# Attention and a gated unit on one core: keys without padding on TensorE's row halves, and turns and casts done by transfers

## The chip, the cores and the metric

One core of one Trainium2 chip. The metric is the device time of one launch in microseconds (us). The kernel before takes 296.35 us, the median of three runs (295.74 to 299.75).

## What is computed

Grouped-query attention over 8 batches, 16 query heads in 4 groups, 384 tokens and 64 numbers per head, and then a gated unit on the heads laid side by side (x, 384 x 1024 per batch):

```python
scores = scale * np.matmul(q, k.transpose(0, 1, 3, 2))
attn = np.exp(scores - max); attn = attn / sum
x = attn @ v                                  # heads side by side: 384 x 1024
h = np.maximum(x @ w_in, 0.0)                 # 1024 -> 1024
u, v = h[..., :512], h[..., 512:]
v_n = (v - mean(v)) / np.sqrt(var(v) + 1e-06)
v_s = einsum('ts,bsd->btd', w_spatial, v_n) + b_spatial[None, :, None]
out = (u * v_s) @ w_out                       # 512 -> 1024
```

Inputs and output are float32; the kernel multiplies in float16 and adds up in float32.

## The kernel before, in words

Tokens are dealt to partitions as token = 3p + t, so that one partition's row of a head is one piece in memory, and three tiles t of 128 tokens make up a sequence.

**Attention.** SP loads q, k and v (L75). POOL casts them to float16 (`cast_k`, `cast_q`, `cast_v`, L177 to L194), batch 0 in part on DVE. TensorE turns k and q by multiplying with an identity, six 128x128 blocks at a time into one PSUM buffer (L205, L225), and DVE copies them out (L216, L235). A pair is two query heads of two neighbouring key groups: head A lies on rows 0 to 63, head B on rows 64 to 127. The keys are kept twice in `kz`, once with zeros on the lower rows and once on the upper, so that a matmul over all 128 rows gives one head's scores. `scores` (L251) does two such matmuls of 384 queries into one PSUM tile, and ACT takes the exp of both at once (L258, 768 columns). 24 such units make a batch. `weigh` (L267) multiplies each 128x128 block of exps with the 64 values and a column of ones; `normalize` (L281, L282) divides by that column on DVE. `x_transposes` (L296) turns x on TensorE and DVE copies it out (L301).

**Gated unit.** `gated_unit` is a generator that yields after each matmul. Per batch: v = x @ w_in for three token tiles (pv, L312, 24 matmuls of 512 columns), relu and statistics on DVE (L321 to L324), u for four column tiles (pu, L332, 32 matmuls of 384 columns) with relu on ACT (L340), normalisation of v on POOL (vn, L350), the product with w_spatial (psp, L362 and L365) in which a matmul of ones with the bias comes first, the product with u on DVE (gT, L373), and out (po, L380, 24 matmuls of 512 columns) that DVE and ACT copy out by halves (L389). SP stores.

**Order.** Scheduling is by hand. The main loop runs over the units n of all batches; each step emits the next unit's scores, the jobs booked with `at(n, ...)`, the weighing that has come due, and as many matmuls of the gated unit of the batch before as a 24th of a batch's columns. Batch 0's gated unit begins at n = 29. Each engine works its queue in that order. The weights w_in and w_out are loaded by SP into three staging buffers (L120, L137) and cast by POOL (L131, L145).

PSUM: two score tiles of two banks, one bank for the weighing, three buffers of one bank (`ps_ck`) for everything else.

Of the kernel before, what the change touches and what calls it, by code (L numbers as in the profile page):

```python
# [17 lines left out]
def kernel(  # L18
# [15 lines left out]
    P = 128  # L34
# [6 lines left out]
    NPAIR = HQ // 2  # L41
# [4 lines left out]
    VW = D + 2  # L46

# [3 lines left out]
    wst = ctx.enter_context(tc.tile_pool(name="wst", bufs=3))  # L51
    ld = ctx.enter_context(tc.tile_pool(name="ld", bufs=2))
    att = ctx.enter_context(tc.tile_pool(name="att", bufs=3))
# [5 lines left out]
    ps_ck = ctx.enter_context(tc.tile_pool(name="ps_ck", bufs=3, space=PSUM))  # L59
# [9 lines left out]
    )  # L69

# [3 lines left out]
    def part(name, src, t, lo, hi, eng=None):  # L74
        (eng or nc.sync).dma_start(  # L75
            t[:, lo:hi, :], src[lo:hi].rearrange("h (p t) d -> p h (t d)", t=NT)
        )

    def stage_tile(n, b, j=None):
        if n == "q":  # L80
            t = ld.tile([P, 2 * G, NT * D], FP32, name=f"q32_{b}_{j}", tag="q32")
            stage[n, b, j] = t
            return t
        t = ld.tile([P, HKV, NT * D], FP32, name=f"{n}32_{b}", tag=f"{n}32")
        stage[n, b] = t
        return t

    def load_k(b):
        part("k", k[b], stage_tile("k", b), 0, HKV)

    def load_v(b):
        part("v", v[b], stage_tile("v", b), 0, HKV)

    def load_q(b, j):
        part("q", q[b, 8 * j : 8 * j + 8], stage_tile("q", b, j), 0, 2 * G)


    k0, v0, q00 = stage_tile("k", 0), stage_tile("v", 0), stage_tile("q", 0, 0)
    part("q", q[0, 0:8], q00, 0, 2, nc.scalar)
    part("k", k[0], k0, 0, 2)  # L100
    part("q", q[0, 0:8], q00, 4, 6)
    part("v", v[0], v0, 0, 2)
    part("q", q[0, 0:8], q00, 2, 4)
    part("q", q[0, 0:8], q00, 6, 8)
    part("k", k[0], k0, 2, 4)
    part("v", v[0], v0, 2, 4)
    load_q(0, 1)

    w_in16 = cst.tile([P, NPAIR, DFF], FP16, name="w_in16")
    w_out16 = cst.tile([P, NM, DM], FP16, name="w_out16")  # L110
    wsT16 = cst.tile([P, NT, S], FP16, name="wsT16")

    w_stage = {}

    def load_w_in(j, half):

        t = wst.tile([P, G, DH], FP32, name=f"wi32_{j}_{half}", tag="w32")
        for hh in range(2):
            r0 = (8 * j + 4 * hh) * D
            nc.sync.dma_start(  # L120
                t[hh * D : (hh + 1) * D],
                moe_w_in[r0 : r0 + G * D, half * DH : (half + 1) * DH].rearrange(
                    "(i d) f -> d i f", i=G
                ),
            )
        w_stage["in", j, half] = t

    def cast_w_in(j, half, engs):
        t = w_stage.pop(("in", j, half))
        for i in range(G):  # L130
            engs[i % len(engs)].tensor_copy(  # L131
                w_in16[:, G * j + i, half * DH : (half + 1) * DH], t[:, i]
            )

    def load_w_out(c):
        t = wst.tile([P, 2, DM], FP32, name=f"wo32_{c}", tag="w32")
        nc.sync.dma_start(  # L137
            t, moe_w_out[2 * c * P : 2 * (c + 1) * P, :].rearrange("(m p) f -> p m f", p=P)
        )
        w_stage["out", c] = t  # L140

    def cast_w_out(c, engs):
        t = w_stage.pop(("out", c))
        for i in range(2):
            engs[i % len(engs)].tensor_copy(w_out16[:, 2 * c + i], t[:, i])  # L145


    ident = cst.tile([P, P], FP32, name="ident")
    make_identity(nc, ident)
    ident16 = cst.tile([P, P], FP16, name="ident16")  # L150
    nc.vector.tensor_copy(ident16, ident)
    eps_t = cst.tile([P, 1], FP32, name="eps_t")
    nc.vector.memset(eps_t, 1e-6)
    kz = [cst.tile([P, 2, 2, S], FP16, name=f"kz{i}") for i in range(2)]
    v1 = [cst.tile([P, HKV, NT, VW], FP16, name=f"v1_{i}") for i in range(2)]
    for i in range(2):
        for j in range(2):
            eng = nc.vector if i == 0 and j == 0 else nc.gpsimd
            eng.memset(kz[i][D:P, 0, j], 0.0)
            eng.memset(kz[i][0:D, 1, j], 0.0)  # L160
        nc.gpsimd.memset(v1[i][:, :, :, D:VW], 1.0)
    ones_b = cst.tile([P, P], FP16, name="ones_b")
    nc.gpsimd.memset(ones_b, 0.0)
    nc.gpsimd.memset(ones_b[0:1, :], 1.0)
    nc.gpsimd.memset(ones_b[32:33, :], 1.0)
    bias_b = cst.tile([P, S], FP16, name="bias_b")
    nc.gpsimd.memset(bias_b, 0.0)


    k16s, q16s = {}, {}  # L170

    def cast_k(b, eng, js=(0, 1)):
        if b not in k16s:
            k16s[b] = ld.tile([P, 2, NT, 2, D], FP16, name=f"k16_{b}", tag="k16")
        src = stage["k", b].rearrange("p (j h) (t d) -> p j h t d", h=2, t=NT)
        for hh in range(2):
            eng.tensor_copy(  # L177
                k16s[b][:, js[0] : js[-1] + 1, :, hh, :], src[:, js[0] : js[-1] + 1, hh]
            )

    def cast_v(b, eng, js=(0, 1)):
        g0, g1 = 2 * js[0], 2 * js[-1] + 2
        eng.tensor_copy(
            v1[b % 2][:, g0:g1, :, 0:D].rearrange("p g t d -> p (g t) d"),
            stage["v", b][:, g0:g1].rearrange("p g (t d) -> p (g t) d", t=NT),
        )

    def cast_q(b, j, eng, parts=1):
        t = ld.tile([P, G, NT, 2, D], FP16, name=f"q16_{b}_{j}", tag="q16", bufs=4)
        src = stage.pop(("q", b, j)).rearrange("p (h i) (t d) -> p h i t d", h=2, t=NT)  # L190
        n = G // parts
        for c in range(parts):
            for hh in range(2):
                eng.tensor_copy(  # L194
                    t[:, c * n : c * n + n, :, hh, :].rearrange("p i t d -> p (i t) d"),
                    src[:, hh, c * n : c * n + n].rearrange("p i t d -> p (i t) d"),
                )
        q16s[b, j] = t


    def k_transposes(b, js=(0, 1)):
        ps = ps_ck.tile([P, len(js), S], FP16, name=f"kps_{b}_{js[0]}", tag="ck")
        for x, j in enumerate(js):
            for t in range(NT):
                nc.tensor.transpose(  # L205
                    ps[:, x, t * P : (t + 1) * P],
                    k16s[b][:, j, t].rearrange("p h d -> p (h d)"),
                    ident16,
                )
        z = kz[b % 2]  # L210
        for hh in range(2):
            dst, src = z[hh * D : (hh + 1) * D, hh, js[0] : js[-1] + 1], ps[hh * D : (hh + 1) * D]
            if b == 0 and js == (0,) and hh:
                nc.scalar.copy(dst, src)
            else:
                nc.vector.tensor_copy(dst, src)  # L216

    qTs = {}

    def q_transposes(b, c):  # L220
        ps = ps_ck.tile([P, 2, S], FP16, name=f"qps_{b}_{c}", tag="ck")
        t16 = q16s[b, c // 2]
        for i in range(2):
            for t in range(NT):
                nc.tensor.transpose(  # L225
                    ps[:, i, t * P : (t + 1) * P],
                    t16[:, 2 * (c % 2) + i, t].rearrange("p h d -> p (h d)"),
                    ident16,
                )
        qT = att.tile([P, 2, S], FP16, name=f"qT_{b}_{c}", tag="qT")  # L230
        if b == 0 and c == 0:
            nc.scalar.copy(qT[:, 0], ps[:, 0])  # L232
            nc.vector.tensor_copy(qT[:, 1], ps[:, 1])
        else:
            nc.vector.tensor_copy(qT, ps)  # L235
        qTs[b, c] = qT


    aTs, avs, x16s, xts = {}, {}, {}, {}

    def scores(n):
        b, r = divmod(n, 24)
        pair, u = divmod(r, 3)
        j = pair // G
        if u == 0:
            aTs[b, pair] = att.tile([P, 6, S], FP16, name=f"aT_{b}_{pair}", tag="aT")
        aT = aTs[b, pair]
        sc = ps_sc.tile([P, 2, 512], FP32, name=f"sc_{b}_{pair}_{u}", tag="sc")
        for i in range(2):
            hh, t = divmod(2 * u + i, NT)  # L250
            nc.tensor.matmul(  # L251
                sc[:, i, 0:S],
                kz[b % 2][:, hh, j, t * P : (t + 1) * P],
                qTs[b, pair // 2][:, pair % 2, :],
                start=True,
                stop=True,
            )
        nc.scalar.activation(aT[:, 2 * u : 2 * u + 2, :], sc[:, :, 0:S], AF.Exp, scale=scale)  # L258
# [45 lines left out]
    def gated_unit(b):  # L304
# [70 lines left out]
        for tt in range(NT):  # L375
# [16 lines left out]
            if not last:  # L392
                nc.sync.dma_start(rows[:, tt, :], osb)
# [164 lines left out]
```

## Time and profile before

| | |
|---|---|
| median of three runs | 296.35 us |
| span of the profiled execution | 297.9 us |
| TensorE busy | 277.2 us (93%) |
| ACT, DVE, POOL busy | 182.7, 164.1, 76.8 us |
| moved by transfers | 38.75 MB, mean 130 GB/s |
| first score matmul starts | 8.46 us |
| last w_in load lands | 43.8 us |
| last po matmul ends | 294.1 us |

The span is from the first to the last instruction of one execution; the runs' times lie around it. A busy share is an average over stages with different limits, so the windows of a stage are read next to it. Matmul ends in the profile are modelled, so that a matmul's mean duration is longer than the pace at which one follows the other; the chain in order of time gives that pace.

### The profile page before, as it was taken

The page shows a single profiled execution, that of the slowest core. Times are in us where ns is not written, and L with a number is a line of the kernel's source. Part 1 is how long each engine was busy: PE and PEld are TensorE (multiplying, and loading weights), DVE is VectorE, ACT ScalarE, POOL GpSimd, SP SyncE. Part 2 cuts the span into 40 slices and gives each one's busy share as a digit, 9 for nine tenths or more (in the row PEclk, how much of TensorE's full clock was granted, in tenths as well). Part 3 has the DMA queues.
Part 4 walks back from the last instruction along what each step waited for, and adds up shares of the span by engine and source line. Part 5 has one row for each costly group of instructions (what it writes and reads, how often), then busy time and mean ns, then how long its engine had stood idle before and what let it go on. Part 6 is the DMA issues. An engine that isn't in the chain of part 4 may idle for free.

```text
span 297.9 us, 6566 instructions
## 1 busy us (share of the span) xinstructions
PE 277.2 (93%) x2745; PEld 174.8 (59%) x2745; DVE 164.1 (55%) x358; ACT 182.7 (61%) x267; POOL 76.8 (26%) x123
## 2 busy tenths in 40 slices
PE   1888766999999999999999999999999999999994
PEld 1566433666566666666566656666566666665451
DVE  4356460556474656656474665656474665646641
ACT  1889632576757666776757666676757666673122
POOL 6433549693004230062003230062003000030030
PEclk9999995999999999999999999999999999999999
DMA  7999999813590037600491036600400032002305
GB/s 222 302 217 215 223 273 379 260 23 123 180 312 8 2 139 214 179 0 28 181 284 44 0 144 207 183 2 18 195 4 0 2 136 78 2 0 78 135 1 211
DMA packets 31951, 38.75 MB, mean 130 GB/s; under 512 B 1201, under 2 KB 25778, under 8 KB 31922
## 3 DMA queue, kind: packets, MB, share of 16 engines
q1 hardware_dynamic: 31650, 38.15, 42.3%
q8 instruction: 21, 0.34, 0.5%
q10 hardware_dynamic: 272, 0.20, 0.2%
q14 instruction: 8, 0.07, 0.1%
HBM read 25.76 MB, written 12.58 MB: 129 GB/s over the span
## 4 chain that ended last, share of the span: by engine, by line
PE 82%; DMA 11%; SPq 3%; POOL 2%; DVE 1%; issue 1%; ACT 0%; DVEq 0%; POOLq 0%
PE sc L251 17%; PE pu L332 14%; PE po L380 14%; PE pv L312 13%; PE av L267 10%; DMA wi<-in_moe_w_in_dram 9%; PE psp L365 5%; PE xps L296 3%; PE qps L225 3%; SPq L75 2%; PE psp L362 2%; POOL w_in L131 1%; DMA q<-in_q_dram 1%; PE kps L205 1%; POOL ws L420 1%; SPq L120 1%
## 5 line engine op out<-in xcount | busy, mean ns | idle before, releaser
L258 ACT ACTIVATE aT<-sc 128x768 f16<-128x768 f32 x192 | 153.5, 810 | 87.3 <-PE sc L251 87.1
L251 PE MATMUL sc<-qT,kz 128*128 128x384 f16 x384 | 95.4, 332 | 3.4 <-ACT qT L232 2.4
L267 PEld LDWEIGHTS <-aT 128*128 128x128 f16 x1152 | 53.4, 98 | 17.1 <-issue 0.7
L267 PE MATMUL av<-v,aT 128*128 128x65 f16 x1152 | 57.2, 194 | 0.0
L350 POOL TENSOR_SCALAR vn<-vr,rstd,nmr 128x512 f16<-128x512 f32 x24 | 18.2, 773 | 150.5 <-DVE nmr L345 130.8
L332 PE MATMUL pu<-xt,w_in 128*128 128x384 f16 x256 | 50.9, 326 | 0.0
L312 PE MATMUL pv<-w_in,xt 128*128 128x512 f16 x192 | 50.8, 386 | 0.0
L380 PE MATMUL po<-w_out,gT 128*128 128x512 f16 x192 | 49.2, 379 | 0.1
L251 PEld LDWEIGHTS <-kz 128*128 128x128 f16 x384 | 34.4, 99 | 23.9 <-issue 3.8
L282 DVE TENSOR_TENSOR x<-av,r 128x384 f16<-128x384 f32 x64 | 35.7, 557 | 2.2
L235 DVE COPY qT<-qps 128x768 f16<-128x768 f16 x31 | 17.1, 551 | 27.0 <-PE qps L225 27.0
L281 DVE RECIPROCAL r<-av 128x6 f32<-128x6 f32 x64 | 12.5, 195 | 34.9 <-PE av L267 33.8
L332 PEld LDWEIGHTS <-w_in 128*128 128x128 f16 x256 | 22.7, 98 | 12.7 <-issue 0.3
L194 POOL CAST q<-q 128x768 f16<-128x768 f32 x30 | 24.0, 830 | 8.0 <-DMA q<-in_q_dram 8.0
L380 PEld LDWEIGHTS <-gT 128*128 128x128 f16 x192 | 16.8, 97 | 15.6 <-DVE gT L373 2.4
L312 PEld LDWEIGHTS <-xt 128*128 128x128 f16 x192 | 16.6, 99 | 13.5 <-issue 0.9
L365 PE MATMUL psp<-wsT,vn 128*128 128x384 f16 x96 | 24.2, 326 | 0.0
L389 DVE COPY osb<-po 128x512 f32<-128x512 f32 x24 | 16.5, 689 | 13.2 <-PE po L380 13.2
L373 DVE TENSOR_TENSOR gT<-psp,uT 128x384 f16<-128x384 f32 x32 | 17.1, 553 | 11.5 <-PE psp L365 11.3
L321 DVE TENSOR_SCALAR vr<-pv 128x512 f32<-128x512 f32 x24 | 16.5, 688 | 12.4 <-PE pv L312 12.2
L301 DVE COPY xt<-xps 128x768 f16<-128x768 f16 x32 | 17.6, 551 | 6.6 <-PE xps L296 5.3
L389 ACT COPY osb<-po 128x512 f32<-128x512 f32 x24 | 14.0, 581 | 10.5 <-PE po L380 10.5
(50 smaller groups left out, 186.6 us busy)
## 6 DMA issues: line engine op xcount, KB each, us to landing
q<-in_q_dram SPq DMA_DIRECT2D x15, 768.0 KB, 8.6
out_dram<-osb SPq DMA_DIRECT2D x21, 512.0 KB, 2.8
wi<-in_moe_w_in_dram SPq DMA_DIRECT2D x8, 512.0 KB, 15.3
k<-in_k_dram SPq DMA_DIRECT2D x7, 384.0 KB, 5.1
v<-in_v_dram SPq DMA_DIRECT2D x7, 384.0 KB, 5.5
wo<-in_moe_w_out_dram SPq DMA_DIRECT2D x2, 1024.0 KB, 13.5
out_dram<-osb SPq DMA_DIRECT2D x6, 256.0 KB, 2.0
q<-in_q_dram SPq DMA_DIRECT2D x3, 192.0 KB, 3.9
```

Of the source, the lines that this page charges most:

```text
L194: eng.tensor_copy(t[:, c * n : c * n + n, :, hh, :].rearrange("p i t d -> p (i t) d"), src[:, hh, c * n : c * n + n].rearrange("p i t d -> ...
L251: nc.tensor.matmul(sc[:, i, 0:S], kz[b % 2][:, hh, j, t * P : (t + 1) * P], qTs[b, pair // 2][:, pair % 2, :], start=True, stop=True,)
L258: nc.scalar.activation(aT[:, 2 * u : 2 * u + 2, :], sc[:, :, 0:S], AF.Exp, scale=scale)
L267: nc.tensor.matmul(av[:, hh, qt, :], aT[:, hh * NT + t, qt * P : (qt + 1) * P], v1[b % 2][:, g, t, 0 : D + 1], start=(t == 0), stop=(t == ...
L282: nc.vector.tensor_tensor(x16s[b][:, :, pair * P : (pair + 1) * P].rearrange("p t (h d) -> p h t d", h=2), av[:, :, :, 0:D], r.to_broadcas ...
L301: nc.vector.tensor_copy(xts[b][:, 2 * c : 2 * c + 2, :], ps)
L312: nc.tensor.matmul(pv, xt[:, kt, st * P : (st + 1) * P], w_in16[:, kt, DH:DFF], start=(kt == 0), stop=(kt == NPAIR - 1),)
L332: nc.tensor.matmul(pu[:, 0:S], w_in16[:, kt, m * P : (m + 1) * P], xt[:, kt, :], start=(kt == 0), stop=(kt == NPAIR - 1),)
L350: nc.gpsimd.tensor_scalar(vn, v_r[st], rstd[:, st : st + 1], nmr[:, st : st + 1], op0=ALU.mult, op1=ALU.add,)
L365: nc.tensor.matmul(psp[:, 0:S], v_n[st][:, m * P : (m + 1) * P], wsT16[:, st, :], start=False, stop=(st == NT - 1),)
L380: nc.tensor.matmul(po, gT[:, m, tt * P : (tt + 1) * P], w_out16[:, m, half * 512 : (half + 1) * 512], start=(m == 0), stop=(m == NM - 1),)
L389: (nc.scalar.copy if half else nc.vector.tensor_copy)(osb[:, cols], po)
```

## The change

- Keys are no longer padded. A set is one tile of 128 queries of four heads in each of two groups. A unit is one tile of 128 keys against 512 queries (four heads) for each of two groups: the one group's keys and queries lie on rows 0 to 63, the other's on rows 64 to 127, and each group's matmul runs over its 64 rows into a PSUM bank of its own. ACT takes the exp of 1024 columns at once. 18 units make a batch, and they are emitted two at a time, so that nine steps make a batch.
- From batch 2 on (for x from batch 1 on) q, k and x are turned by SP's transposing transfers from SBUF to SBUF (`k_send`, `q_send`, `x_send`); so is w_spatial. Batches 0 and 1 are still turned on TensorE.
- w_in and w_out are loaded and cast in one transfer each part, issued by POOL, straight into the float16 tiles; the staging buffers and POOL's casts go.
- The bias is spread to all partitions by a transfer and added by DVE (`vs`); the product with u moves to POOL. The bias matmuls go.
- The statistics enter POOL's normalisation as mean and rstd, so that DVE's step for the negative product goes.
- po is copied out by DVE alone, but for the last batch.
- Batch 0's gated unit begins within batch 0, by token tiles; the others wait for step 7 and step 11 of their batch (the `("from", n)` yields).
- PSUM: `ps_av` takes two banks, `ps_ck` has two buffers instead of three.

```diff
+    SETS = 2 * NT
+    UNITS = NT * SETS
+    STEPS = UNITS // 2
...
-    ps_ck = ctx.enter_context(tc.tile_pool(name="ps_ck", bufs=3, space=PSUM))
+    ps_ck = ctx.enter_context(tc.tile_pool(name="ps_ck", bufs=2, space=PSUM))
...
+    def load_w_in(half, lo, hi):
+        cols = slice(half * DH, (half + 1) * DH)
+        pool.dma_start(
+            w_in16[:, lo:hi, cols],
+            moe_w_in[lo * P : hi * P, cols].rearrange("(t p) f -> p t f", p=P),
+        )
...
+    def k_send(b):
+        new_kT(b)
+        sp.dma_start_transpose(
+            kTs[b].rearrange("p j (t c) -> p (j t) c", t=NT),
+            k16s[b].rearrange("p j t h d -> p (j t h d)"),
+        )
+
+    def q_send(b, j):
+        new_qT(b, j)
+        sp.dma_start_transpose(
+            qTs[b, j].rearrange("p t (i c) -> p (t i) c", i=G),
+            q16s[b, j].rearrange("p t i h d -> p (t i h d)"),
+        )
...
+    def unit(u):
+        b, r = divmod(u, UNITS)
+        s, kt = divmod(r, NT)
+        qt, j = divmod(s, 2)
...
+        sc = ps_sc.tile([P, 2, G * P], FP32, name=f"sc_{b}_{s}_{kt}", tag="sc")
         for hh in range(2):
+            rows = slice(hh * D, (hh + 1) * D)
             nc.tensor.matmul(
+                sc[:, hh, :],
+                kTs[b][rows, j, kt * P : (kt + 1) * P],
+                qTs[b, j][rows, qt, :],
                 start=True,
                 stop=True,
             )
+        act.activation(aTs[b, s][:, kt], sc, AF.Exp, scale=scale)
...
+    def x_send(b, qt):
+        if qt == 0:
+            new_xt(b)
+        sp.dma_start_transpose(
+            xts[b][:, :, qt * P : (qt + 1) * P], x16s[b][:, qt]
+        )
...
+        if b == 0:
+            for st in range(NT):
+                yield ("from", 3 * st + 5)
+                yield from v_part(st)
+                if st == NT - 1:
+                    norm()
+                yield from u_part(st)
+        else:
+            yield ("from", b * STEPS + 7)
+            yield from v_part(0)
+            yield from v_part(1)
+            yield ("from", b * STEPS + 11)
+            yield from v_part(2)
+            yield from u_cols()
...
-            nc.tensor.matmul(psp[:, 0:S], ones_b, bias_b, start=True, stop=False)
-            yield S
...
-            nc.vector.tensor_tensor(gT[:, m, :], psp[:, 0:S], uT[:, m, :], ALU.mult)
+            vs = moe.tile([P, S], FP32, name=f"vs_{b}_{m}", tag="vs", bufs=4)
+            dve.tensor_tensor(vs, psp[:, 0:S], bias_bc, ALU.add)
+            pool.tensor_tensor(gT[:, m, :], vs, uT[:, m, :], ALU.mult)
...
+    for b in range(2, B):
+        s0 = STEPS * b
+        at(s0 - 12, load_k, b)
+        at(s0 - 12, load_v, b)
+        at(s0 - 11, load_q, b, 0)
+        at(s0 - 10, load_q, b, 1)
+        at(s0 - 8, cast_k, b, pool)
+        at(s0 - 7, cast_q, b, 0, pool)
+        at(s0 - 6, k_send, b)
+        at(s0 - 5, q_send, b, 0)
+        at(s0 - 5, cast_q, b, 1, pool)
+        at(s0 - 3, q_send, b, 1)
+        at(s0 - 2, cast_v, b, pool)
...
+    for n in range(total + 1):
+        for u in (2 * n, 2 * n + 1):
+            if u < UNITS * B:
+                unit(u)
...
+        sets = ends.pop(n, [])
+        owed = pour(n, owed + STEP - len(sets) * WEIGH)
+        for b, s in sets:
+            weigh(b, s)
+            if s % 2 and b:
+                x_send(b, s // 2)
```

`v_part`, `u_part` and `u_cols` emit pv and pu, the first by token tiles and the last by column tiles. With a step's units come the jobs booked for it, then the gated unit's matmuls, then the weighing that has come due. The order of TensorE's queue in a steady batch is, for the stretch that the prediction speaks of: the sixth weighing, a burst of two units, three and eight pv matmuls, a burst, the eight pv matmuls of the third token tile.

## The prediction

> **What bounds the kernel now.** I read the totals first, then the strip of slices, then the windows of one steady batch, and last the chain of waits inside that batch. The totals put the span at 297.9 us; 297.9 is 1.5 us above the median of the runs shown (296.35), so my sum is made against the span and 1.5 us is taken off at the end.
>
> ```profile
> PE 277.2 (93%) x2745; PEld 174.8 (59%) x2745; DVE 164.1 (55%) x358; ACT 182.7 (61%) x267; POOL 76.8 (26%) x123
> ...
> PE   1888766999999999999999999999999999999994
> ...
> PEclk9999995999999999999999999999999999999999
> DMA  7999999813590037600491036600400032002305
> GB/s 222 302 217 215 223 273 379 260 23 123 180 312 8 2 139 214 179 0 28 181 284 44 0 144 207 183 2 18 195 4 0 2 136 78 2 0 78 135 1 211
> ```
>
> From the eighth slice to the end TensorE has no gap, while transfers have many. Before that, transfers are full and TensorE is not: the load of inputs and weights sets the first 50 us. The windows, one per batch, show the steady part (PE, weight loads, DVE, ACT, POOL, clock, transfer share, GB/s):
>
> ```profile
> 44.70:57.00 12.30, 8.95 (x64) 5.20 (x65) 3.65 (x9) 3.27 (x5) 11.99 (x17) 0.72 1.00 333
> ...
> 109.60:143.17 33.57, 33.57 (x344) 21.46 (x342) 19.98 (x43) 22.64 (x34) 7.10 (x10) 1.00 0.37 119
> 143.17:176.74 33.57, 33.57 (x344) 21.47 (x342) 19.97 (x43) 22.64 (x34) 7.10 (x10) 1.00 0.38 119
> ```
>
> A batch takes 33.57 us and all of it is TensorE. ACT and DVE have 11 and 14 us to spare. The chain in order of time gives the pace of each kind of matmul without the modelled ends:
>
> ```profile
> 143.17 0.86 PE po L380 x4
> 144.04 0.33 PE sc L251 x2
> ...
> 145.33 0.28 PE av L267 x9
> ...
> 146.48 0.34 PE qps L225 x6
> ```
>
> So 512 columns cost 0.216 us, 384 columns 0.163, a 65-column product 0.0315, a 128-column turn 0.056. One batch: scores 48 x 0.163 = 7.8, weighing 144 x 0.0315 = 4.5, pv and po 24 x 0.216 = 5.2 each, pu 32 x 0.162 = 5.2, psp 16 x 0.162 = 2.6, turns 54 x 0.056 = 3.0; the sum, 33.5, is the measured 33.57. Eight batches are 268.5 us of the 297.9; 29 us are the start, waits before 57 us, and the tail.
>
> **The change, part by part.**
>
> Turns. Of 441 turns on TensorE 84 stay (q and k of batches 0 and 1, x of batch 0): 4.7 us instead of 24.7, so -20.0. In their place SP issues 40 turning transfers. DVE loses the copies behind the turns, ACT and POOL nothing.
>
> Bias. Four matmuls per batch go: 32 x 0.162 = -5.2. The addition moves to DVE in the instruction's place that multiplied (553 ns each), and the product with uT goes to POOL.
>
> Scores. 288 matmuls of 512 columns carry the same 147,456 columns as 384 of 384, now on 64 rows, two at a time on the two row halves. No row shows two matmuls at once. Serial, they cost 288 x 0.216 = 62.2 us, no gain; wholly side by side, 31.1. I take side by side, because the halves differ in rows, keys, queries and PSUM banks, plus one uncovered weight load at each of the 72 bursts (99 ns mean of the kz loads): 31.1 + 7.1 = 38.2, that is 0.53 us for a burst of two units, -24 against 62.2. Ends: 31.1 and 62.2 + 14 (a load uncovered on the way in and on the way out). Two rules of the Trainium skill bear on it: TensorEngine Tiling (Array Packing), Key Properties, says that a change of tiling mode drains the engine, which speaks against 144 changes; TensorE: Matmul & The Clock Gate, Part 3, says that tiles on different row groups overlap and gives 3.07x for four of them. An estimate from that, 62.2 / (2 x 0.77) = 40.5 us, would put my sum 2 us higher. No trace here shows either.
>
> Work that is left: (17.5 of gated unit + 4.5 weighing + 4.8 scores) x 8 + 4.7 = 219 us against 268.5.
>
> Other engines per batch. ACT: the exp rises from 768 to 1024 columns; 487 ns at 384 and 810 at 768 make 0.84 ns a column, so 1.03 us: 18 x 1.03 + 4 x 0.487 + 0.5 = 20.9 us. DVE: six normalisations of about 0.92, three of pv (0.69 + 0.70 + 0.18), four additions, six copies of po (ACT's three are moved here): 16.5. POOL: casts 5.2, vn 2.3, four products; for these the rows are 508 ns (cast of 384) and 1002 ns (the only tensor-tensor of POOL, on one partition); I take 0.8: 10.7. None reaches 27. SP: 13 issues per batch, seven plain ones at 0.45 us (the timeline's issue of k_0 and its neighbours) and six turning ones without a row, between 0.45 and the 2.8 that a whole store takes to land: 6 to 20 us, below 27 at both ends. SP also waits in order: an x transfer that waits for its normalisation holds the stores and the next batch's q and k behind it, and these are needed four steps or more later.
>
> Weights. The casts of w_in and w_out on POOL (13.2 us) and the staging buffers go. But the first gated unit is moved up: its pu stands behind 14 units of batch 0, where the kernel before had finished most of two batches' attention. TensorE's queue is in order, so the scores behind pu wait for w_in's second half. Until w_in has landed 2.4 MB of batch 0 and 4.2 MB of w_in must come, and SP's queue runs ahead with batch 1 (2.4 MB), the spatial weights and keys of batch 2 (1.6 MB) on the same engines. At 240 GB/s (the first 29 us) the 6.6 MB alone take 27 us, all 10.6 MB 44; with about 3 us before the first byte that is 30 to 47, and I take 37. The nearest row agrees in size: the last w_in load before lands at 43.8 us. Until then TensorE does 14 units (3.7), 38 turns (2.1), three weighings (2.3) and one pv (1.7), 9.8 us. So 27 us of the start are no work. The first score's wait for all eight heads instead of four (some 2 us at 220 GB/s) and POOL's six weight issues (0.45 each, as SP's) lie inside this wait and cost nothing; if w_in came early they would cost 2 and up to 3. After the 4.9 us wait before, the clock stood at 0.72 through 12.3 us, a loss of 3.4; I charge 3.
>
> New waits in a steady batch. (a) The last x transfer. pv of the third token tile stands 3.4 us behind the end of the sixth weighing (two bursts 1.06, three and eight pv matmuls 2.4), and needs normalisation and semaphores (about 1.1) and the transfer of 256 KB. Rows: a 256 KB store lands in 2.0 us, a 512 KB one in 2.8, a 768 KB load in 8.6 in company. I take 2.8, the next row up from its own size, as stores and loads run beside it: 0.5 us each, seven times. Ends: 0 and 6.3. Behind it wait the next bursts, and ACT behind them. (b) Two PSUM buffers instead of three: psp's second column group needs the buffer that ACT empties after two exps (2.06) and its own 0.49; the step's own work is 0.8 us shorter. I take 0.8; ends 0 and 1.3. (c) gT now passes DVE (0.55) and POOL (0.8) before po: the second po matmul is 0.4 late. Ends 0 and 1. Together 1.7 x 7 = 12.
>
> ```profile
> L350 POOL TENSOR_SCALAR vn<-vr,rstd,nmr 128x512 f16<-128x512 f32 x24 | 18.2, 773 | 150.5 <-DVE nmr L345 130.8
> ...
> q<-in_q_dram SPq DMA_DIRECT2D x15, 768.0 KB, 8.6
> out_dram<-osb SPq DMA_DIRECT2D x21, 512.0 KB, 2.8
> wi<-in_moe_w_in_dram SPq DMA_DIRECT2D x8, 512.0 KB, 15.3
> ...
> out_dram<-osb SPq DMA_DIRECT2D x6, 256.0 KB, 2.0
> ```
>
> Tail. The x transfer of batch 7 has a burst less to hide behind (1.5 exposed), the gT products in line expose 2.2 more than psp covers, and from the last po matmul to the end it is 3.8 as before: 7.5.
>
> Sum: 219 + 27 + 3 + 12 + 7.5 = 268.5 in span; less 1.5, 267.
>
> **Rivals.** First, the turning transfers set the pace. One mechanism: the 256 KB of x land as late as the 768 KB loads, 8.6 us, and pv waits 6.3 instead of 0.5 in seven batches: +41, 308 us, slower than before. It decides from a landing of 7.8 us (slower by 2%); from 6.1 there is no gain to measure. For it: turning moves two-byte elements, no row shows one, and 1.8 MB more per batch use the same engines. Against it: transfers are at 0.37 of their time in a steady batch, and q and k go out four to six steps (11 us or more) ahead. The Trainium skill has two figures that disagree: VectorE: DVE Perf Modes, The three transpose paths, has 1309 ns for a 128x128 block, so eight in line would take 10.5 us, an estimate that makes 321; DMA: Bandwidth & Descriptors, Latency and other measured facts, has 261 GB/s, so 1 us of data. No run here shows either yet.
>
> Second, the row halves don't run at once: scores stay at 62.2 + 7.1, +31, 298: no change. For it: no row shows concurrency, and the kernel before pays full price for zero rows. Against it: weight loads overlap matmuls throughout (21.5 us of them inside a full 33.57).
>
> Third, the waits don't come: w_in lands at 32 us, transfers land in 2 us, bursts take 0.45: -5 - 12 - 6, 244. For it: ACT and DVE have slack, and a wait in one place covers the next. Against it: each engine's queue is in order.
>
> **How the numbers follow.** Forecast 267, its own range 252 to 286: chance 0.60. Transfers set the pace, 308: 0.15. Halves serial, 298: 0.08. No waits, 244: 0.17. A measurement of this kernel tells about 2% from no change, 290.4 to 302.3. Faster: 0.60 + 0.17 = 0.77; within: 0.08; slower: 0.15. The range, 244 to 298, takes in the forecast and the second and third rival and leaves out the first, with some 0.03 for an end of the third below 244.
>
> **What would show it.** Scores: pairs of matmuls in the timeline with starts closer than 0.2 us, a burst near 0.53 us; serial if the 288 take 62 in the chain. Start: a wait of pu on transfers until about 37 us. Turning transfers: their time to landing, 2 to 4 us if right, over 7.8 if the first rival holds, and the wait of pv's weight load on DMA. Batch period: 28.5 us; above 32 the gain is gone. I am wrong most easily in the time of the transfers, the start, and the sum of small waits.

## The result and the profile after

The changed kernel takes 314.5 us, the median of four runs (311.8 to 318.6), against 297.0 us for the kernel before: a ratio of 1.053 (95% interval 1.044 to 1.062), slower. The prediction was 267 us, so it is wrong in sign. The profiled execution took 311.8 us with a span of 310.0. Times here are medians of all runs, and ratios leave out runs more than 1.5% above a kernel's fastest; the one such run of the changed kernel raises its median by 0.5 us, and with it each gain counted from 314.5.

First the page of the changed kernel: busy totals, and the strips of TensorE, its granted clock and the transfers.

```profile
PE 253.5 (82%) x2324; PEld 129.0 (42%) x2324; DVE 137.7 (44%) x269; ACT 159.1 (51%) x196; POOL 124.2 (40%) x134
...
PE   2797885896597986979698995979798999897865
...
PEclk9999998699899995999989996899999999999979
DMA  7999994089507992359904896159905550134005
```

TensorE has less work, and it is no longer full: the unbroken nines of the kernel before have become nines, eights and sevens with a fall to 5 or 6 about once a batch, and the clock falls too (mean 0.950 against 0.989). POOL's busy time has risen by 47 us, though its weight casts are gone.

The windows of three batches (columns as before: PE, weight loads, DVE, ACT, POOL, clock, transfers, GB/s). The first two still have loads for a later batch in them, the third has none.

```profile
171.35:207.63 36.28, 31.26 (x273) 15.47 (x273) 16.32 (x32) 19.47 (x25) 14.60 (x15) 0.91 0.64 158
207.63:239.87 32.24, 28.68 (x273) 14.47 (x273) 16.30 (x32) 19.47 (x25) 14.60 (x14) 1.00 0.70 178
239.87:270.79 30.92, 28.68 (x273) 14.48 (x273) 16.31 (x32) 19.47 (x25) 10.52 (x9) 1.00 0.32 88
```

The same matmuls take 36.3 and 32.2 us a batch with loads and 30.9 without, 28.5 by the prediction, 33.57 before. The two windows with loads differ in the clock: 0.91 in the one, 1.00 in the other, whose x transfer landed sooner (4.43 us). The chain in order of time shows where the first window goes (start, us, what):

```profile
182.88 0.54 PE sc L221 x4
183.42 0.46 PE pv L289 x2
183.88 5.97 DMA xt<-x
...
189.90 3.60 PE pv L289 x8
...
204.61 0.50 PE psp L370 x2
```

POOL's timeline has the three normalisations that come just ahead of that psp:

```profile
198.36 6.19 POOL L310 TENSOR_SCALAR vn<-vr,mv,rstd 128x512 f16<-128x512 f32 x3 [14.64 <-ACT rstd L307]
```

A burst of two units takes 0.54 us, as predicted. But the third x transfer takes 5.97 us, and after it eight pv matmuls take 3.60 us instead of 1.73. Further on psp waits for three normalisations on POOL of some 2.07 us each, 6.19 us together; over the whole run these waits of psp come to 14.7 us. These are the two places.

### The profile page after: what moved, and what is told of

Read it like the earlier page. It is cut to its first block, busy times and chain, and to the rows that moved or that the text cites. A ratio compares the mean times of both kernels' runs of the same rounds, so it can differ in the third digit from the quotient of the medians.

```text
span 310.0 us, 5653 instructions
## 1 busy us (share of the span) xinstructions
PE 253.5 (82%) x2324; PEld 129.0 (42%) x2324; DVE 137.7 (44%) x269; ACT 159.1 (51%) x196; POOL 124.2 (40%) x134
## 4 chain that ended last, share of the span: by engine, by line
PE 38%; POOL 20%; DMA 17%; issue 16%; ACT 4%; DVE 3%; SPq 1%; POOLq 1%; DVEq 0%; ACTq 0%
PE po L387 13%; POOL vn L310 12%; DMA xt<-x 9%; PE pv L289 9%; PE av L237 8%; PE sc L221 6%; DMA v_None<-in_v_dram 5%; POOL gT L380 3%; ACT aT L228 3%; PE psp L370 2%; DVE vs L379 2%; DMA k_None<-in_k_dram 1%; POOL q L158 1%; ACT uT L348 1%; POOL q L163 1%
## 5 line engine op out<-in xcount | busy, mean ns | idle before, releaser
L228 ACT ACTIVATE aT<-sc 128x1024 f16<-128x1024 f32 x144 | 139.3, 1022 | 118.1 <-PE sc L221 118.1
L310 POOL TENSOR_SCALAR vn<-vr,mv,rstd 128x512 f16<-128x512 f32 x24 | 49.5, 2070 | 112.7 <-ACT rstd L307 95.7
L289 PE MATMUL pv<-w_in,xt 128*128 128x512 f16 x192 | 52.5, 421 | 19.7 <-DMA xt<-x 19.7
L221 PE MATMUL sc<-qT,kT 64*128 64x512 f16 x288 | 46.8, 397 | 3.6 <-ACT aT L228 3.0
L237 PE MATMUL av<-v,aT 128*128 128x65 f16 x1152 | 46.1, 197 | 0.0
L379 DVE TENSOR_TENSOR vs<-psp,bias_bc 128x384 f32<-128x384 f32 x32 | 17.3, 557 | 53.9 <-PE psp L370 53.3
L399 DVE COPY osb<-po 128x512 f32<-128x512 f32 x45 | 31.1, 691 | 16.1 <-PE po L387 14.9
L370 PE MATMUL psp<-wsT,vn 128*128 128x384 f16 x96 | 23.6, 360 | 17.1 <-POOL vn L310 14.7
L249 DVE TENSOR_TENSOR x<-av,r 128x512 f16<-128x512 f32 x48 | 33.2, 691 | 1.7
L380 POOL TENSOR_TENSOR gT<-vs,uT 128x384 f16<-128x384 f32 x32 | 28.6, 912 | 7.4 <-DVE vs L379 7.2
L348 ACT ACTIVATE uT<-pu 128x384 f16<-128x384 f32 x28 | 13.9, 495 | 13.3 <-PE pu L340 12.7
L298 DVE TENSOR_SCALAR vr<-pv 128x512 f32<-128x512 f32 x24 | 16.5, 686 | 6.2 <-PE pv L289 5.9
L300 DVE BATCH_NORM_STATS2 stats<-vr 128x6 f32<-128x512 f32 x24 | 16.7, 695 | 0.8
```

Source lines behind the costliest of these rows:

```text
L221: nc.tensor.matmul(sc[:, hh, :], kTs[b][rows, j, kt * P : (kt + 1) * P], qTs[b, j][rows, qt, :], start=True, stop=True,)
L228: act.activation(aTs[b, s][:, kt], sc, AF.Exp, scale=scale)
L237: nc.tensor.matmul(av[:, hh, i * (D + 1) : (i + 1) * (D + 1)], aT[:, kt, hh, i * P : (i + 1) * P], v1[b % 2][:, 2 * j + hh, kt, 0 : D + 1] ...
L249: dve.tensor_tensor(x16s[b][:, qt, j * 512 : (j + 1) * 512].rearrange("p (h i d) -> p h i d", h=2, i=G), o[:, :, :, 0:D], r.to_broadcast([ ...
L289: nc.tensor.matmul(pv, xt[:, kt, st * P : (st + 1) * P], w_in16[:, kt, DH:DFF], start=(kt == 0), stop=(kt == NK - 1),)
L310: pool.tensor_scalar(vn, v_r[st], mv[:, st, 0:1], rstd[:, st : st + 1], op0=ALU.subtract, op1=ALU.mult,)
```

## The experiments

Each kernel's edit is against the changed kernel unless said otherwise. The kernels that were run together ran on one chip, with the kernel before beside them. There were several such sessions, and the changed kernel was timed in one of its own; the kernel before had medians of 297.0 to 298.7 us in them, so 1 or 2 us between kernels of different sessions tell nothing.

**POOL's normalisation.** The group of the changed kernel stands at 2070 ns, where the kernel before had 773:

```profile
L310 POOL TENSOR_SCALAR vn<-vr,mv,rstd 128x512 f16<-128x512 f32 x24 | 49.5, 2070 | 112.7 <-ACT rstd L307 95.7
```

Same tile, same types; the operations differ.

```diff
+            nmr = small.tile([P, NT], FP32, name=f"nmr_{b}", tag="nmr")
+            dve.scalar_tensor_tensor(
+                nmr, mv[:, :, 0], -1.0, rstd, op0=ALU.mult, op1=ALU.mult
+            )
...
-                    mv[:, st, 0:1],
                     rstd[:, st : st + 1],
-                    op0=ALU.subtract,
-                    op1=ALU.mult,
+                    nmr[:, st : st + 1],
+                    op0=ALU.mult,
+                    op1=ALU.add,
```

> The changed kernel with POOL's normalisation of v as before: v times rstd plus nmr (multiply, add), with nmr made by one small DVE instruction, instead of v minus mean times rstd (subtract, multiply). Theory: the form of the instruction makes it 2.07 us instead of 0.77; here it falls back to 0.77, the waits of psp on POOL fall from 14.7 us to under 4, and the time by 12 to 18 us, to 296 to 302. Rival: POOL is slowed by what else runs beside it (turning transfers, DVE); then the instruction stays at 2.07 and the time within 3 us of 314.

Measured: 303.5 us, 11.0 less than the changed kernel; ratio to the kernel before 1.019 (1.012 to 1.027). The group, by form:

```profile
L314 POOL TENSOR_SCALAR vn<-vr,rstd,nmr 128x512 f16<-128x512 f32 x24 | 18.1, 767 | 112.0 <-DVE r L248 58.8 <-DVE nmr L309 36.3 <-PE pu L344 16.9
```

The instruction is back at its old duration with the same turning transfers beside it, so the contention rival falls. The gain is 1 us short of the expected range.

**The loads ahead of the x transfer.** SP's own timeline of the changed kernel, ahead of the transfer that took 5.97 us, shows two loads of q and three stores:

```profile
175.75 0.58 SPq L84 DMA_DIRECT2D q<-in_q_dram  x1
176.43 0.58 SPq L403 DMA_DIRECT2D out_dram<-osb  x1
177.05 0.43 SPq L84 DMA_DIRECT2D q<-in_q_dram  x1
178.61 3.55 SPq L403 DMA_DIRECT2D out_dram<-osb  x2
183.88 1.29 SPq L272 DMA_TRANSPOSE xt<-x  x1
```

The edit moves the loads and nothing else:

```diff
-        at(s0 - 12, load_k, b)
-        at(s0 - 12, load_v, b)
-        at(s0 - 11, load_q, b, 0)
-        at(s0 - 10, load_q, b, 1)
+        at(max(s0 - 17, 6), load_k, b)
+        at(max(s0 - 17, 6), load_v, b)
+        at(max(s0 - 15, 7), load_q, b, 0)
+        at(max(s0 - 13, 8), load_q, b, 1)
```

> The changed kernel with the loads of k, v and q of a later batch issued 3 to 5 steps earlier, so that none of them stands on SP's queue shortly before the third x transfer; the bytes are the same. Theory: that transfer lands late (4.4 to 6 us from issue) because loads and stores ahead of it have not drained; with only stores ahead it lands in 3 to 4 us, the waits of pv on transfers fall from 19.7 us to under 10, the granted clock rises from 0.95 to 0.97 or more, and the time falls by 8 to 16 us, to 298 to 306. Rival: the turning itself takes that long; then landing, waits and time stay, 311 to 317.

Measured: 294.3 us, 20.2 less than the changed kernel and more than expected; ratio to the kernel before 0.990 (0.982 to 0.997). Waits of pv on transfers fell from 19.7 to 7.0 us and the clock rose to 0.974. Its chain, at the same place of a batch:

```profile
171.77 0.46 PE pv L289 x2
172.24 3.10 DMA xt<-x
...
175.38 1.90 PE pv L289 x8
```

The same 256 KB now land in 3.10 us, and pv runs at its pace again. So the turning is not slow by itself; the loads issued ahead of it made it late. They slowed the stores as well: a store of 512 KB took 6.1 us to land in the changed kernel (median), 2.7 here and 2.8 in the kernel before. Whether the x transfer waits its turn in SP's queue or shares the transfer engines with the loads was not separated. Windows of the changed kernel around the wait show both sides of it:

```profile
179.00:190.00 11.00, 7.54 (x81) 3.66 (x78) 6.07 (x12) 5.81 (x6) 1.60 (x2) 0.94 1.12 310
190.00:201.00 11.00, 11.00 (x88) 5.86 (x89) 3.27 (x7) 5.03 (x8) 2.64 (x2) 0.75 0.05 10
```

In the stretch that ends with TensorE's wait, transfers run at 310 GB/s; when it may go on they are nearly empty, and the clock has a mean of 0.75 over 11 us, which is another 2.8 us on top of the 3.5 of the wait. The Trainium skill (TensorE: Matmul & The Clock Gate, Part 1) puts the idle window after which the clock falls at about 3.4 us. The trace does not bear out that length as a limit: 3.46 us idle lowered the clock, but so did 3.04 us a batch earlier (clock 0.53 over the 3.6 us behind it) and 2.39 us in batch 1, behind two shorter waits (eight pv matmuls take 3.51 us there instead of 1.90):

```profile
82.91 3.51 PE L289 MATMUL pv<-w_in,xt 128*128 128x512 f16 x8 [2.39 <-DMA xt<-x]
```

Waits of 1.92 and 1.70 us in this kernel, and of 0.72 in the kernel with both edits below, left the clock at 1.00.

**x on TensorE.**

```diff
             if s % 2 and b:
-                x_send(b, s // 2)
+                at(n + 1, x_turn, b, s // 2, dve.tensor_copy)
```

> The changed kernel with x of all batches turned on TensorE, as batch 0's is, and no x transfer. It adds 168 turns of 0.056 us (9.4 us) to TensorE and 21 copies to DVE. Theory: the waits for x (19.7 us of pv idle, and the clock that they lower, some 8 to 12 us) are worth more than the turns: 292 to 302. Rival: the waits merely hide others (POOL's normalisation, the loads): then the turns are paid on top, 312 to 322.

Measured: 301.3 us, 13 less than the changed kernel; ratio to the kernel before 1.012 (1.004 to 1.020). So the x transfers as they were scheduled cost more than the turns that they replace.

**Both edits, and x on TensorE on top of them.** The edits of the first two experiments, together:

> The changed kernel with both: POOL's normalisation as multiply and add, and the loads issued earlier. Theory: the two waits lie at different places of a batch (psp on POOL, pv on the x transfer) and add up: 11 and 20 us of 314.5, so 280 to 288, with waits of psp on POOL under 5 us and of pv on transfers under 9. Rival: what the one frees the other takes, because a later engine (DVE, ACT) is then late: 290 to 295.

Measured: 281.9 us, ratio to the kernel before 0.955 (0.943 to 0.967). Of 11.0 + 20.2 us alone, 32.6 come together. The two waits add up; together they turn the change from 5% slower to 4.5% faster.

> As e5_both, with x of all batches turned on TensorE. Theory: once nothing stands ahead of it, the x transfer costs a wait of about 1 us a batch, less than the 1.34 us of TensorE and the waits for DVE's copy: e5_both plus 2 to 10. Rival: the transfer still costs more than the turns: e5_both less 2 or more.

Measured: 293.2 us, 11.3 more than with the transfers, and 1.3 above the expected range; ratio to the kernel before 0.995 (0.992 to 0.999). The chain shows what a turn on TensorE brings beside its own 0.41 us: it waits for the normalisation ahead of it, and po behind it waits for the copy.

```profile
191.24 0.70 DVE x L249
...
191.99 0.41 PE xps L266 x4
192.43 0.70 DVE xt L267
```

So undoing "x by transfer" is worth -13 us where the loads stand ahead of it and the normalisation is slow, and +11 us where both are mended. That it is the loads that decide the sign is argued from the landing times above and not shown, as loads and normalisation were not varied one without the other here. The Trainium skill (VectorE: DVE Perf Modes, The three transpose paths) has 1309 ns for a block of 128x128. Here eight blocks took 3.1 us, landing included, which is 0.39 us each, so that figure is not one to multiply by the number of blocks.

**The row halves alone, on the kernel before.** Keys unpadded, a unit's two heads on the two halves, and the weighing one step later:

```diff
-            hh, t = divmod(2 * u + i, NT)
+            rows = slice(i * D, (i + 1) * D)
             nc.tensor.matmul(
                 sc[:, i, 0:S],
-                kz[b % 2][:, hh, j, t * P : (t + 1) * P],
-                qTs[b, pair // 2][:, pair % 2, :],
+                kT[b % 2][rows, j, u * P : (u + 1) * P],
+                qTs[b, pair // 2][rows, pair % 2, :],
...
-        if n % 3 == 2 and n - 2 < total:
-            weigh(*divmod((n - 2) // 3, NPAIR), 0)
         if n % 3 == 0 and 0 < n <= total:
-            weigh(*divmod((n - 3) // 3, NPAIR), 1)
-            normalize(*divmod((n - 3) // 3, NPAIR))
+            weigh(*divmod((n - 3) // 3, NPAIR), 0)
+        if n % 3 == 1 and 1 < n <= total + 1:
+            weigh(*divmod((n - 4) // 3, NPAIR), 1)
+            normalize(*divmod((n - 4) // 3, NPAIR))
```

> The kernel before with one part of the change alone: unpadded keys, each pair's two heads on the two row halves, 384 queries, one pair of matmuls at a time (not in bursts of two units), and the weighing one step later; turns, casts, bias and gated unit as before. Theory: two matmuls run at once, a pair costs 0.165 to 0.2 us instead of 0.33, and as TensorE is the bound all of it shows: 296 less 24 to 31, 265 to 273. Rival: entering and leaving the half-row mode costs something at each of the 192 pairs, 0.1 us or more; then 285 or above.

Measured: 312.3 us, ratio 1.052 (1.044 to 1.060): slower, a clear miss. The chain of this kernel:

```profile
143.37 0.27 PE sc L241 x2
143.64 0.39 PE av L259 x9
```

A pair takes 0.27 us, not 0.33, so the two do run at once, at least in part. But it is not 0.163, and nine weighing matmuls behind it take 0.39 instead of 0.28. Together 0.66 against 0.61: 0.05 us lost at each of 192 pairs, 9 or 10 us of the 12.7 by which the span grew. The rest can be from the weighing's new place (po waits 3.3 us for DVE here, not before); that was not separated.

**The same price in the changed kernel.** Two variants of the kernel with both edits: score matmuls over all 128 rows, and bursts of one unit.

```diff
-            rows = slice(hh * D, (hh + 1) * D)
+            rows = slice(0, P)
```

> As e5_both, but both score matmuls of a unit run over all 128 rows, as with padded keys, instead of over 64; nothing else differs. The rows of both groups are summed in the scores, so the numbers of the attention are other ones; the instructions' sizes are those of a padded kernel. Theory: a burst on the row halves takes 0.54 us and the matmuls after it 0.18 more than their pace, 0.72 together, against 0.86 for four full matmuls, so 72 bursts are worth only 10 us: e5_both plus 7 to 13. Rival: the halves are worth what two at once promise (0.86 against 0.43 to 0.53): plus 24 or more.

```diff
-        for u in (2 * n, 2 * n + 1):
-            if u < UNITS * B:
-                unit(u)
+        if 2 * n < UNITS * B:
+            unit(2 * n)
...
-        owed = pour(n, owed + STEP - len(sets) * WEIGH)
+        due = owed + STEP - len(sets) * WEIGH
+        owed = pour(n, due / 2)
+        if 2 * n + 1 < UNITS * B:
+            unit(2 * n + 1)
+        owed = pour(n, owed + due / 2)
```

> As e5_both, but the two units of a step are emitted half a step apart, so that 144 bursts of one unit take the place of 72 of two. Theory: each change into and out of the half-row mode costs 0.1 us and 0.18 us, so 72 more bursts cost 20 us: e5_both plus 14 to 24, and slower than the padded form of e7_full_rows. Rival: a burst has no fixed cost, the 0.18 us is the exp or a wait: within 5 us of e5_both.

Measured: 290.7 us with full rows (8.9 more than the halves) and 292.3 with one-unit bursts (10.4 more, less than the 14 to 24 expected). The chain with full rows and then the one with one-unit bursts:

```profile
177.81 0.86 PE sc L221 x4
178.68 1.79 PE pu L344 x11
```

```profile
177.63 0.32 PE sc L221 x2
177.96 1.08 PE pu L344 x6
```

The kernel with full rows adds up both groups' rows in each score, so its attention is another one, while its instructions have the sizes of a padded kernel. With full rows, eleven pu matmuls behind the burst take 1.79 us, their pace of 11 x 0.162. Behind a half-row burst eleven take 1.89 in the kernel with both edits, and six take 1.08 instead of 0.97 here: 0.10 or 0.11 more, not the 0.18 that I had read from po's groups, which have 0.08 of their own with full rows too. So a burst costs: one unit 0.32 + 0.11 = 0.43, two units 0.54 + 0.10 = 0.64, a pair of 384 columns 0.27 + 0.11 = 0.38. Less the columns at two at once (0.216, 0.432, 0.163), each leaves 0.21 or 0.22 us. One price fits all three: half of it before the columns, half after. Against full matmuls (0.43, 0.86, 0.33) a burst of one unit wins nothing, one of two wins 0.22, a pair of 384 loses 0.05. "In bursts of two" is what makes the halves pay at all.

The whole times move by less than this price. The 72 bursts win 16 us of work, of which 8.9 show: with full rows pv's waits are 3.6 us instead of 7.0, and the clock is 0.994 instead of 0.985. The 72 more bursts of the other variant should cost 15 us, of which 10.4 show, at a clock of 0.994 too; what covers the rest was not taken apart. The Trainium skill (TensorEngine Tiling (Array Packing), Key Properties) says that a change of mode drains the engine. The runs fit that, as they show a fixed price for each burst; they do not tell a drain from weight loads that nothing covers (two of 0.099 us would come to nearly the same).

**The other parts.** The bias as before, on the kernel with both edits:

```diff
+            nc.tensor.matmul(psp[:, 0:S], ones_b, bias_b, start=True, stop=False)
+            yield C384
...
-            vs = moe.tile([P, S], FP32, name=f"vs_{b}_{m}", tag="vs", bufs=4)
-            dve.tensor_tensor(vs, psp[:, 0:S], bias_bc, ALU.add)
-            pool.tensor_tensor(gT[:, m, :], vs, uT[:, m, :], ALU.mult)
+            dve.tensor_tensor(gT[:, m, :], psp[:, 0:S], uT[:, m, :], ALU.mult)
```

> As e5_both, with the bias part undone: a matmul of ones with the bias ahead of each psp group, and the product with u on DVE straight from PSUM; POOL's product and DVE's addition go. TensorE gets 32 x 0.162 = 5.2 us back. Theory: the waits of psp and po on DVE and POOL in e5_both (2.1 + 2.4 us in the queue, some 1.5 of it in the tail) and the longer tail are worth about as much: within 3 us of e5_both. Rival: DVE and POOL's chain is covered, and the matmuls are paid in full: plus 5 or more.

Measured: 283.0 us, ratio to the kernel before 0.956 (0.946 to 0.966): no difference that can be told. The 5.2 us of matmuls and the chain through DVE and POOL (a product of 912 ns there) come to about the same.

Which part of POOL's instruction was slow:

```diff
-                    op0=ALU.subtract,
+                    op0=ALU.add,
                     op1=ALU.mult,
```

(the scalar being the mean times -1).

> As e5_both, with POOL's normalisation as v plus minus-mean, times rstd (add, multiply): the order of the changed kernel without its subtraction. Theory: subtraction is what makes the instruction 2.07 us; here it takes 0.77. Rival: it is the order (an addition ahead of the multiplication): 2.07.

Measured: 281.3 us in its one run, and

```profile
L312 POOL TENSOR_SCALAR vn<-vr,nmr,rstd 128x512 f16<-128x512 f32 x24 | 18.1, 766 | 133.2 <-ACT rstd L307 133.2
```

The order of the changed kernel is kept and only the subtraction is an addition, so it is the subtraction that was slow.

The weights by POOL's transfers, alone on the kernel before:

```diff
-            nc.sync.dma_start(
-                t[hh * D : (hh + 1) * D],
+            nc.gpsimd.dma_start(
+                w_in16[hh * D : (hh + 1) * D, G * j : G * j + G, half * DH : (half + 1) * DH],
...
-    at(17, cast_w_in, 0, 1, (pool,))
-    at(21, cast_w_in, 1, 1, (pool,))
```

> The kernel before with one part of the change alone: w_in and w_out loaded and cast by POOL's transfers straight into the float16 tiles, at the places in the order where SP loaded them; no staging and no casts of weights on POOL. Theory: the wait for the second half of w_in and behind it w_spatial (TensorE idle from 42 to 47 us, clock 0.72 after it) shrinks, since POOL's 13 us of weight casts no longer stand ahead of w_spatial's: 286 to 293. Rival: the first 50 us are bound by bytes: within 3 us of the kernel before.

Measured: 290.8 us, ratio 0.985 (0.975 to 0.995): a gain of some 4 to 6 us, which the interval lets be as small as 1.5. The 4.9 us wait of w_spatial's turns is gone and the clock is 1.000 instead of 0.989.

**A better version.** With both edits, pv of the third tile still waits 0.72 us a batch for a transfer that lands 3.2 us after its issue. The weighing that is due in that step goes ahead of it:

```diff
+        due = owed + STEP - len(sets) * WEIGH
+        early_weigh = n % STEPS == 2 and n > STEPS
+        if not early_weigh:
+            owed = pour(n, due)
         for b, s in sets:
...
+        if early_weigh:
+            owed = pour(n, due)
```

> As e5_both, but in the step in which pv of the third token tile comes, the weighing that is due in that step (0.75 us) goes ahead of it instead of behind it. Theory: in e5_both pv waits 0.7 us a batch for an x transfer that lands 3.2 us after its issue, and 0.75 us of work put ahead covers it: less 3 to 5 us, 277 to 279. Rival: pv's results are then later by as much for DVE, ACT and POOL, and the next wait (psp, 0.6 us on ACT) grows by what this one loses: within 1.5 us of e5_both.

Measured: 276.5 us, ratio to the kernel before 0.933 (0.926 to 0.940), the fastest here, and a little more of a gain than the 3 to 5 us expected. TensorE's timeline now has no wait between the two:

```profile
194.91 0.92 PE L237 MATMUL av<-v,aT 128*128 128x65 f16 x24
195.74 1.90 PE L289 MATMUL pv<-w_in,xt 128*128 128x512 f16 x8
```

## Why the prediction was wrong, point by point

**What bounded the kernel before** was right: work taken off TensorE shows in good part, once nothing else is late.

**The third x transfer** is the step that failed most. The prediction took 2.8 us, the time of a store, "0.5 us each", with 6.3 as the far end, and gave the late landing as the first rival with a chance of 0.15, needing 7.8 us to decide the sign. The landing came to 4.4 to 6.4 us in four batches, less than 7.8. But I priced the wait alone, and a wait of 3.5 us also cost the clock, some 2.8 us more. What I had not looked at is what SP issues just ahead of the transfer: 2.4 MB of loads and 1.5 MB of stores within 12.5 us. My argument against the rival was a share, transfers at 0.37 of their time, and a share over a batch says nothing of the moment: with both edits a batch has shares up to 0.74 and the transfer still lands in 3.2 us. Moving the loads gave back 20.2 us. That alone leaves the kernel about level with the one before (0.990), so the loss has further terms.

**POOL's normalisation** was put down as "vn 2.3" a batch, from the row of 773 ns. The diff changes its operations and the trace of before has no subtraction on POOL with a whole tile, so it had to be bounded; I took the row as if the instruction were the same. Nor is psp's wait for it among the new waits of the prediction, which put it at nothing; it measured 14.7 us. It cost 11.0 us alone, 12.4 beside the moved loads.

**The row halves**: the mechanism was right, the size was not. I put one uncovered weight load of 0.099 us at a burst, and kept two as the far end; the price is 0.21, near that of two, and the term is 46 us, not 38.2, against 62.2. That is 8 us; the rival that the halves don't run at once is dead.

**The start** was too long: pu's wait for w_in was 0.57 us at 26.2 us, not until 37. That is near the 30 us at which only the bytes of batch 0 and of w_in come first; the four w_in transfers landed in 8.6 us each, where the eight loads of the row before took 15.3. Why they land sooner was not separated. The start took some 11 us off the sum, and hid as much of the other errors; that the total was not further off is luck.

**Turns, bias, copies, ACT and DVE** fit: with both edits a batch takes 30.3 us against 28.5, of which 0.9 is the second half of the bursts' price, 0.2 the rest of the x wait, and some 0.7 was not taken apart. ACT and DVE are busy 19.5 and 16.4 us of it, 20.9 and 16.5 by the prediction. The turns of q and k were not undone by themselves. The bias was: the prediction took 5.2 us off for its matmuls and charged 2.8 + 2.2 for the longer chain to po, nothing in sum, as measured. The small waits, priced at 1.2 us (psp on ACT, po on POOL), measure 1.06 (0.63 + 0.23 + 0.20).

**Sum.** 267 as predicted, + 32.6 for the loads and the subtraction, + 8 for the bursts, - 11 for the start, makes 297; measured is 314.5. Some 18 us are left. Some 7 to 9 of them lie between the gT products of batch 0 and batch 1: in the kernel with both edits the first ones start 37.3 us apart and the last ones end 39.0 apart, against 30.3 later. There the gated unit waits for its step, TensorE has only scores for a while, ACT's exp sets the pace, and a wait of 2.23 us for x lowers the clock. The remaining part was not taken apart.

## What to carry to other kernels

Before a transfer is put on the path, list what is issued just ahead of it at that moment; here the same transfer landed in 3.1 us or in 6.0, and moving the loads that stood ahead was worth 20 us. An instruction whose operation changes is a new instruction: it needs its own row or a bound, even if shape and engine stay. Matmuls on row halves pay per burst, so count bursts and not matmuls, and put as much as PSUM holds into each.

## What the runs showed of the hardware

- POOL's tensor-scalar on 128x512: 2070 ns with a subtraction, 766 to 773 with add and multiply in either order.
- A burst of half-row matmuls among matmuls over all rows has a fixed price of 0.21 us, about half before and half after it, at 384 and 512 columns, one pair or two.
- A turning transfer of 256 KB occupies SP's queue for 1.23 us, where a plain one takes 0.4 to 0.9, and lands in 3.0 to 3.7 us in the kernel with both edits, in 4.4 to 6.4 in the changed kernel where 2.4 MB of loads stand just ahead of it.
- 3.46 us without matmuls lowered TensorE's clock to 0.50 for the next 3.5 us and to 0.61 for 2.5 more, a mean of 0.75 over 11 us; 3.04 and 2.39 us lowered it too, 1.92 and 1.70 did not.
